# A gated recurrence and its MLP on one core: the recurrence's late chunks on 64x64 tiles only, in three steps with a VectorE copy between them, and a new order of the steps

## The chip, the cores and the metric

One NeuronCore of a Trainium2 chip runs the program. The metric is the device time of one execution in microseconds (us); before the change it is 501.38 us, the median of 3 runs (501.32 to 502.95). Engines are named TensorE (PE in the profile, its weight loads PEld), VectorE (DVE), ScalarE (ACT), GpSimd (POOL) and SyncE (SP, which issues the DMAs).

## The reference

Two stages follow each other. The first is a gated linear recurrence over 768 time steps for 4 batches of 8 heads of width 48, the second an MLP with a Mish activation over all 3072 tokens of width 384, with 2048 hidden units:

```python
# recurrence (B=4, H=8, S=768, D=48), f = sigmoid(f_logit)
for t in range(S):
    state = f[:, :, t, :, None] * state + einsum('bhd,bhe->bhde', k[:, :, t], v[:, :, t])
    y[:, :, t] = einsum('bhd,bhde->bhe', q[:, :, t], state)
x = y.transpose(0, 2, 1, 3).reshape(B * S, H * D)      # 3072 x 384
# MLP
h = x @ w_in                                            # 3072 x 2048
g = h * tanh(log1p(exp(h)))
out = g @ w_out                                         # 3072 x 384
```

## The kernel before

**The recurrence in chunks.** A chunk is 128 time steps of one batch; there are 24 (n = 0 to 23), four of which (one of each batch) make the 512 tokens of one group g of the MLP. Within a chunk the work is done in halves of 64 steps. For a chunk TensorE forms the scores of keys and queries (`score`, L525), which VectorE multiplies with a causal mask into the tiles `a` (`mask`, L532); the two states' updates from keys and values (`update`, L568), from which VectorE makes `mid` (L627) and `tmp` (L629) and GpSimd the next state (L717); and the output `y`, a sum in PSUM of what the state brings (`inter_at`, L691) and of what the masked scores bring within the chunk (`intra_at`, L699). Each of these products uses a part of TensorE's array: a row tile of 64 rows (which half of the partitions the operands lie on) and a column tile (which half of the partitions of PSUM the result goes to). Each fp32 matmul stands as two records in the trace.

**Late chunks.** From n = 9 (`MERGED`) on, that is for 15 chunks, the output of chunk n-1 and the scores and updates of chunk n are issued as one run on TensorE, in `attn2`. It is made of two steps that follow each other at once (`plan.glue(1)`): `run` issues the products `near(1 - e, e, ..., 32)` on tiles of 64 rows by 32 columns, then 16 `far` products on 64x64 tiles in turn with 16 scores; `run_on` issues the other half of `far` and scores, the updates and the products `near(e, e)`. `far` is `inter_at`, `near` is `intra_at`. `near(c, e)` works on row tile c and adds to PSUM bank `y[e]`, `far(e, ...)` works on row tile e and adds to the same bank. `y` lies in banks `at_[0]` and `at_[1]`, and so do the updates (their second halves); the scores lie in `at_[2]` (`at1`) and in `h_[lent]`, the one of the MLP's two h banks that is lent for it.

**The MLP.** For each unit u (group g, hidden block j of 128) TensorE makes h in 9 matmuls of 512 columns (`moe_in`, L261), then ScalarE, VectorE and GpSimd turn it into `gh` and `gl` (`mish`, L277 to L292; the order is exp L285, +1 L286, square L278, ln L288, exp L289, times h L290, split L292 and L282), and two units later TensorE adds 9 matmuls to the four output banks `o_` (`moe_out`, L299). The first blocks use plain fp32 (L269, L272).

**The order.** `Plan` collects all steps with an engine and a cost written by hand, packs them by a list schedule, searches for an order by repeated forward and backward packings and then by random changes of the ranks (`order`, 10 settings with 30 turns each, then `SHIFTS` = 1000 draws), and issues every engine's instructions in that order. Each engine runs its own instructions strictly in it. At the start `issue` fills TensorE's waiting time with matmuls on zeros (`idle`, L402).

Of the kernel before, what the change touches and what calls it, by code (L numbers as in the profile page):

```python
# [10 lines left out]
F32 = mybir.dt.float32  # L11
# [10 lines left out]
P = 128  # L22
# [21 lines left out]
EARLY = 24  # L44
EARLY_J = 2
WHOLE = 5
SHIFTS = 1000
MERGED = 2 * GC + 1


class Plan:
# [30 lines left out]
    def pack(self, rank, ahead, haste, back=False):  # L82
# [20 lines left out]
        forced = None  # L103
        found = dict.fromkeys(queue)
        stale = set(queue)
        transfers = shared = 0.0
        for _ in range(count):
            for e in stale:
                found[e], q, at_least = None, queue[e], free[e]
                if q:  # L110
                    at = [(max(ready[i], shared) if port[i] else ready[i], i) for i in q]
                    t0 = max(at_least, min(at)[0])
                    _, t, i = min(
                        [(rank[i] + haste * max(0.0, r - t0), max(at_least, r), i) for r, i in at if r <= t0 + ahead]
                    )
# [12 lines left out]
            end = free[e] = t + cost[i]  # L128
            if port[i]:
                shared = end  # L130
                stale.update(("dve", "pool"))
            if e == "sp" and not back:
                transfers = max(transfers, end + 650.0) + steps[i][4] / 0.27
                end = transfers - 650.0
            for a in after[i]:
                f = a if back else i
                if engine[i] == engine[a] == "pe":
                    lag = 0.0
                else:
                    lag = self.LATENCY[engine[f]]  # L140
                    if back and engine[f] == "sp":
                        lag += steps[f][4] / 0.27
                ready[a] = max(ready[a], end + lag)
                left[a] -= 1
                if not left[a]:
                    queue[engine[a]].append(a)
                    stale.add(engine[a])
        return start

    def order(self):  # L150

        count = len(self.steps)
        cost = [s[1] for s in self.steps]

        def packed(rank, *setting):
            start = self.pack(rank, *setting)
            return max(start[i] + cost[i] for i in range(count)), start

        best = None
        for setting in ((200.0, 5.0), (400.0, 10.0), (1000.0, 20.0), (200.0, 50.0), (50.0, 2.0), (0.0, 0.0), (100.0, 1.0), (100.0, 20.0), (300.0, 20.0), (600.0, 20.0)):  # L160
            rank = list(range(count))
            for _ in range(30):
                end, start = packed(rank, *setting)
                if best is None or end < best:
                    best, self.start, kept = end, start, (rank, setting)
                back = self.pack([-start[i] - cost[i] for i in range(count)], *setting, True)
                rank = [-back[i] - cost[i] for i in range(count)]
        ranks, setting = kept
        draw = random.Random(1)
        for _ in range(SHIFTS):  # L170
            spread, width = draw.choice((200, 500, 1500, 4000)), draw.choice((5e3, 2e4, 1e5, 5e5))
            left = draw.random() * best * 0.3
            rank = [r + (draw.gauss(0, spread) if left <= at < left + width else 0) for r, at in zip(ranks, self.start)]
            end, start = packed(rank, *setting)
            if end <= best:
                best, self.start, ranks = end, start, rank
        return sorted(range(count), key=lambda i: (self.start[i], i))

    def issue(self):
# [32 lines left out]
def recurrence_moe_kernel(  # L212
# [18 lines left out]
    def ctile(shape, dtype, name):  # L231
        return const.tile(shape, dtype, tag=name, name=name)
# [15 lines left out]
    ones = ctile([P, 1], F32, "ones")  # L248
    okc = ctile([P, 1], F32, "okc")
    flag = ctile([1, 1], I32, "flag")  # L250
    ends = ctile([P, NCH, NP, 1], F32, "ends")
    state = ctile([P, B, NP, 64], F32, "state")
    state0 = ctile([P, P], F32, "state0")
# [48 lines left out]
    with tc.tile_pool(name="work", bufs=1) as pool, tc.tile_pool(  # L302
# [94 lines left out]
        waits = iter([None] * 26 + [(F32R, P, GT)] * 4 + [(F32R, P, GT // 2)] * 4 + [(BF16, P, GT)] * 4 + [(F32R, 96, GT)] * 4)  # L397

        def idle():
            form = next(waits, None)  # L400
            if form is None:
                nc.tensor.matmul(zeros[:, 0:P], state0[:, 0:P], state0[:, 0:P], start=True, stop=True)  # L402
            else:
                dtype, m, n = form
                z = blank.bitcast(dtype)
                nc.tensor.matmul(zeros[0:m, 0:n], z[:, 0:m], z[:, 0:n], start=True, stop=True)


        def load_w(j):

# [92 lines left out]
        def half(e):  # L503
            return slice(64 * e, 64 * e + 64)
# [10 lines left out]
        def attn0(n, parts):  # L515
# [1 line left out]
            (_, kk_, kq, _), (_, k, q, _), _ = inputs(n)  # L517
            b, keys = taken[n]
            st = NP // parts
            sc = [quad(x) for x in (b if n < MERGED else (at1, h_[lent]))]  # L520
            if n >= MERGED:
                keys = [("at", 2), ("h", lent)]

            def score(e, c, p):
                nc.tensor.matmul(  # L525
# [31 lines left out]
        def attn2(n):  # L557
# [6 lines left out]
            keys = [("at", 0 if merged else 2), ("at", 1)]  # L564
            tmp, kt = tmp_[n % 2], ("tmp", n % 2)

            def update(p, c, e):
                nc.tensor.matmul(  # L568
                    u[c][dims(e), p].rearrange("p (r m) -> p r m", m=4)[:, :, :3],
                    kt_s[half(c), p, dims(e)], v[half(c), 2 * p + e, :, :3],  # L570
                    start=not merged, stop=True, tile_position=(64 * c, 64 * e), skip_group_check=merged,
                )

            def updates():
# [5 lines left out]
            if merged:  # L580
                attn0(n, 1)
                score, mask, reads, writes = late[n]
                old_reads, far, near, rest = outputs_of(n - 1)

                def slot(*calls):
                    for x in range(2):
                        for f, *where in calls:
                            f(*where, x)

                def scored(e, p, x):  # L590
                    score(e, x, p)

                def run():
                    for a in range(2):
                        for x in range(4):
                            for e in (1, 0):
                                near(1 - e, e, a, x, 32)

                    for p in range(NP):
                        slot((far, 0, p // 2, p % 2), (scored, 1, p))  # L600

                def run_on():
                    for p in range(NP):
                        slot((scored, 0, p), (far, 1, p // 2, p % 2))
                    updates()
                    for a in range(2):
                        slot((near, 0, 0, a), (near, 1, 1, a))

                add("pe", 890, run, ["kt", kv[0]] + reads + old_reads, [("at", 0), ("at", 1)] + writes)
                plan.glue(1)  # L610
                add("pe", 1267, run_on, ["kt", kv[0]] + reads[: 2 * NP] + old_reads, [("at", 0), ("at", 1), writes[0]])
                mask()
            elif n >= GC:
                score, mask, reads, writes = late[n]
# [16 lines left out]
                rest()  # L631

        def attn3(n):
            outputs_of(n)[3](True)

        def outputs_of(n):
            (_, _, kq, kv), (_, _, q, v), _ = inputs(n)
# [58 lines left out]
            def intra_at(c, e, a, x, m=64):  # L696
                p = 2 * a + x * m // 64
                c0 = (2 * p + e) * 64 + x * m % 64
                nc.tensor.matmul(  # L699
                    y[e][x * m : x * m + m, a, half(c)], v[half(c), c0 : c0 + m], a_[e][half(c), p, :],  # L700
                    start=(m == 32 and a == 0), stop=True, skip_group_check=True,
                )

            def rest(alone=False):
# [48 lines left out]
            return reads, inter_at, intra_at, rest  # L753


        def start(n):
# [301 lines left out]
```

## Time and profile before

| what | value |
|---|---|
| median of 3 runs | 501.38 us (501.32 to 502.95) |
| the profiled execution's own time | 501.84 us |
| its span, first to last instruction | 500.1 us |
| PE busy | 487.8 us (98%) |
| PEld busy | 390.5 us (78%) |
| ACT busy | 360.0 us (72%) |
| DVE busy | 336.5 us (67%) |
| POOL busy | 143.7 us (29%) |
| granted TensorE clock, mean | 0.996 |

The profile shows one execution. The profiled execution took 501.84 us, of which the span of its instructions is 500.1 us; what is read from rows is counted against these two. A busy time of TensorE holds the latency of its last matmul as well, because matmuls overlap: the distance from the start of one record to the start of the next is what a record costs in a stream, and the text works with these distances. In a timeline, a row with x32 is 32 records that follow each other, with the start of the first and the time to the end of the last.

### The profile page before, as it was taken

What the parts mean: (1) busy time and instruction counts of PE and PEld (TensorE: products, weight loads), DVE (VectorE), ACT (ScalarE), POOL (GpSimd) and SP (SyncE); (2) the same over time, 40 slices, a digit from 0 to 9 for tenths busy, and PEclk for the clock granted to TensorE, in tenths of its full rate; (3) what the DMA queues carried; (4) which work ended last, traced back from release to release, by engine and by line L of the source; (5) the groups of instructions that cost most, each with busy time, mean ns of one, the idle gap of its engine ahead of it and who ended that gap; (6) DMA issues with size and microseconds to landing.
All of it is one profiled execution on the core that took longest, in us unless ns stands there. A gap on an engine that the chain in (4) does not pass through costs nothing.

```text
span 500.1 us, 12645 instructions
## 1 busy us (share of the span) xinstructions
PE 487.8 (98%) x5270; PEld 390.5 (78%) x5270; DVE 336.5 (67%) x585; ACT 360.0 (72%) x662; POOL 143.7 (29%) x128
## 2 busy tenths in 40 slices
PE   8899999999999999999999999999999999999995
PEld 8775557887877888788888888888888888888883
DVE  5579999999968877786666675666664453545441
ACT  7789988999986876777857757767665565655550
POOL 1411210000023443443434324334323223332421
PEclk9999999999999999999999999999999999999998
DMA  7886655542402525122031131130230000010001
GB/s 249 245 259 220 219 200 188 179 170 78 122 0 87 199 102 183 75 93 84 4 118 65 47 124 34 53 118 8 78 108 1 0 2 33 22 43 0 1 0 69
DMA packets 17105, 48.46 MB, mean 97 GB/s; under 512 B 2000, under 2 KB 2000, under 8 KB 17040
## 3 DMA queue, kind: packets, MB, share of 16 engines
q1 hardware_dynamic: 17040, 47.59, 28.3%
q8 instruction: 42, 0.69, 0.6%
q14 instruction: 23, 0.19, 0.1%
HBM read 39.32 MB, written 6.29 MB: 91 GB/s over the span
## 4 chain that ended last, share of the span: by engine, by line
PE 84%; DMA 7%; DVE 4%; ACT 2%; issue 1%; SPq 0%; ACTq 0%; DVEq 0%
PE o L299 38%; PE h L261 37%; DMA raw<-ww 3%; DMA in<-qv 3%; PE at L699 2%; PE at L691 2%; PE at L525 1%; PE at L552 1%; PE at L568 1%; DMA spareh<-qv 1%; PE h L269 1%; DMA spareh<-lk 1%; DVE wt L422 1%; DVE wl L437 1%; ACT wt L419 1%
## 5 line engine op out<-in xcount | busy, mean ns | idle before, releaser
L261 PE MATMUL h<-xt,wh 128*128 128x512 f32 x546 | 171.6, 396 | 0.1
L282 POOL TENSOR_TENSOR gl<-ng,gh 128x512 fp32r<-128x512 f32 x74 | 101.9, 1378 | 194.2 <-ACT gh L292 170.5
L261 PEld LDWEIGHTS h<-xt,wh 128*128 128x128 f32 x546 | 101.2, 188 | 23.5 <-DVE ng L290 1.6
L290 DVE SCALAR_TENSOR_TENSOR ng<-ng,h 128x512 f32<-128x512 f32 x91 | 62.4, 687 | 72.4 <-ACT ng L289 71.5
L299 PE MATMUL o<-gh,wh 128*128 128x512 f32 x273 | 109.4, 401 | 0.4 <-issue 0.4
L261 PE MATMUL h<-xt,wl 128*128 128x512 f32 x273 | 107.4, 393 | 0.1
L299 PE MATMUL o<-gl,wh 128*128 128x512 f32 x273 | 107.3, 393 | 0.0
L299 PE MATMUL o<-gh,wl 128*128 128x512 f32 x273 | 106.5, 390 | 0.0
L288 ACT ACTIVATE ng<-ng,half 128x512 f32<-128x512 f32 (+1 forms) x98 | 69.8, 712 | 48.1 <-DVE ng L278 42.2
L285 ACT ACTIVATE ng<-h 128x512 f32<-128x512 f32 (+1 forms) x98 | 57.4, 586 | 38.0 <-PE h L261 36.6
L286 DVE TENSOR_SCALAR ng<-ng 128x512 f32<-128x512 f32 (+1 forms) x98 | 48.9, 499 | 51.3 <-ACT ng L285 50.8
L292 ACT ACTIVATE gh<-ng 128x512 fp32r<-128x512 f32 x91 | 56.6, 624 | 18.3 <-PE o L299 16.0
L289 ACT ACTIVATE ng<-ng 128x512 f32<-128x512 f32 (+1 forms) x98 | 60.6, 619 | 1.8
L345 POOL TENSOR_TENSOR in<-in,inv 128x512 f32<-128x512 f32 x20 | 24.8, 1242 | 125.7 <-ACT inv L491 119.1
L261 PEld LDWEIGHTS h<-xt,wl 128*128 128x128 f32 x273 | 51.3, 188 | 12.2 <-DVE wl L437 0.6
L299 PEld LDWEIGHTS o<-gl,wh 128*128 128x128 f32 x273 | 51.3, 188 | 11.8 <-DVE gl L281 0.2
L299 PEld LDWEIGHTS o<-gh,wl 128*128 128x128 f32 x273 | 51.3, 188 | 11.2 <-issue 0.6
L299 PEld LDWEIGHTS o<-gh,wh 128*128 128x128 f32 x273 | 51.3, 188 | 10.9 <-DVE ob L845 0.2
L278 DVE TENSOR_TENSOR ng<-ng 128x512 f32<-128x512 f32 x74 | 52.5, 709 | 2.1
L485 DVE TENSOR_TENSOR_SCAN inv<-gate,state 128x516 f32<-128x516 f32 x20 | 26.7, 1334 | 2.7 <-ACT gate L476 1.2
L742 ACT ACTIVATE xt<-at 128x256 fp32r<-128x256 f32 x40 | 13.5, 374 | 5.9 <-PE at L699 4.9
L419 ACT ACTIVATE wt<-raw 128x768 f32<-128x768 f32 x16 | 14.7, 919 | 3.6 <-DMA raw<-ww 3.6
(145 smaller groups left out, 572.0 us busy)
## 6 DMA issues: line engine op xcount, KB each, us to landing
in<-lk SPq DMA_DIRECT2D x18, 512.0 KB, 5.1
raw<-ww SPq DMA_DIRECT2D x12, 768.0 KB, 4.2
in<-qv SPq DMA_DIRECT2D x18, 512.0 KB, 3.7
out<-ob SPq DMA_DIRECT2D x18, 256.0 KB, 2.2
raw<-ww SPq DMA_DIRECT2D x8, 384.0 KB, 4.4
in<-lk SPq DMA_DIRECT2D x8, 256.0 KB, 3.8
in<-qv SPq DMA_DIRECT2D x8, 256.0 KB, 4.2
xt<-xt SPq DMA_DIRECT2D x15, 128.0 KB, 3.5
```

Of the source, the lines that this page charges most:

```text
L261: nc.tensor.matmul(h, w[:, a * P : (a + 1) * P], xt[:, x, a, cols], start=(n == 0), stop=(n == 3 * NK - 1))
L278: ("dve", T_DVE(w), 1, lambda: nc.vector.tensor_tensor(n, n, n, ALU.mult))
L282: ("pool", T_POOL(w), 1, lambda: nc.gpsimd.tensor_tensor(gl, g, gh.bitcast(F32), ALU.subtract))
L285: ("act", T_ACT(w, True), 0, lambda: nc.scalar.activation(n, h, AF.Exp)),
L286: ("dve", T_DVE(w / 2), 1, lambda: nc.vector.tensor_scalar(n, n, E_CAP, 1.0, ALU.min, ALU.add)),
L288: ("act", T_ACT(w, False, 1), 0, lambda: nc.scalar.activation(g, n, AF.Ln, bias=half1, scale=0.5)),
L289: ("act", T_ACT(w), 0, lambda: nc.scalar.activation(g, g, AF.Exp, scale=-1.0)),
L290: ("dve", T_DVE(w), 0, lambda: nc.vector.scalar_tensor_tensor(gw if whole else g, g, 1.0, h, ALU.subtract, ALU.mult)),
L292: ("act", T_ACT(w), 0, lambda: nc.scalar.activation(gh, g, AF.Copy)),
L299: nc.tensor.matmul(o, w, x, start=(first and i == 0), stop=(last and i == 2))
L345: add("pool" if on_pool else "dve", cost, lambda: eng.tensor_tensor(dst, x, y, ALU.mult), reads, writes, port=port)
L485: add("dve", 2 * T_DVE(w + st) - 70, lambda s=s, st=st: nc.vector.tensor_tensor_scan(inv1[:, s].rearrange("p a c -> p (a c)"), gate[:, s]. ...
```

## The change

The late chunks' run is cut into three steps, and all its products use 64x64 tiles. `carried` issues the 16 `far` products and the 8 `near(e, e)`. `scored` issues the 16 scores and the updates and follows `carried` at once on TensorE. `crossed` issues the 8 products `near(1 - e, e)`, now with 64 columns, and follows `scored` at once. Between `carried` and `crossed` stands a step of VectorE, `fence`: a copy of two numbers of `y[0]` on one partition into a new tile `mark`. It waits for `carried`, and `crossed` waits for it. The scores and the updates now share the banks `h_[lent]` and `at1`, so the mask and `mid` of the one bank, and the mask and `tmp` of the other, read from there. The first product to clear the banks `y` is `far` in place of `near`.

In `Plan`, a glued step now holds only its own engine. The search is another: one setting, 30 turns, then a list of draws by seeds, each followed by two turns. `idle` issues only its first form, and a memset of GpSimd for the other forms is gone. The diff, cut:

```diff
-SHIFTS = 1000
+SETTING = (400.0, 10.0)
+MOVES = (
+    300004, 300007, 300012, 300015, 300033, 300038, 300042, 300061, 300072, 300076, 300080, 300084, 300085,
...
+)
...
                 found[e], q, at_least = None, queue[e], free[e]
+                if e in held:
+                    q = [i for i in q if i == held[e]]
...
-            if forced is None:
-                t, i = min(f for f in found.values() if f)
-            else:
-                i = forced
-                t = max(free[engine[i]], ready[i])
-            forced = follower.get(i)
+            t, i = min(f for f in found.values() if f)
             e = engine[i]
+            held.pop(e, None)
+            if i in follower:
+                held[e] = follower[i]
...
+        plan = best = packed(list(range(count)))
+        for _ in range(29):
+            plan = turned(plan[2])
+            if plan[0] < best[0]:
+                best = plan
+        for seed in MOVES:
+            draw = random.Random(seed)
+            spread, width = draw.choice((200, 500, 1500, 4000, 8000)), draw.choice((5e3, 2e4, 1e5, 5e5))
+            end, ranks, start = best
+            left = draw.random() * 0.4 * end
+            plan = best = packed(
+                [r + (draw.gauss(0, spread) if left <= at < left + width else 0) for r, at in zip(ranks, start)]
+            )
+            for _ in range(2):
+                plan = turned(plan[2])
+                if plan[0] < best[0]:
+                    best = plan
...
-        blank = xt_[1][:, 0, 0]
-        nc.gpsimd.memset(blank.bitcast(F32), 0.0)
...
-            sc = [quad(x) for x in (b if n < MERGED else (at1, h_[lent]))]
+            sc = [quad(x) for x in (b if n < MERGED else (h_[lent], at1))]
...
-            u = [quad(at_[0] if merged else at1, NP * 64 * merged), quad(at_[1], NP * 64)]
+            u = [quad(h_[lent], NP * 64), quad(at1, NP * 64)] if merged else [quad(at1), quad(at_[1], NP * 64)]
...
-                def run():
-                    for a in range(2):
-                        for x in range(4):
-                            for e in (1, 0):
-                                near(1 - e, e, a, x, 32)
-                    for p in range(NP):
-                        slot((far, 0, p // 2, p % 2), (scored, 1, p))
-
-                def run_on():
-                    for p in range(NP):
-                        slot((scored, 0, p), (far, 1, p // 2, p % 2))
+                def carried():
+                    for c in range(2):
+                        for a in range(2):
+                            for x in range(2):
+                                for e in range(2):
+                                    far(e, c, a, x)
+                    for a in range(2):
+                        for x in range(2):
+                            for e in (1, 0):
+                                near(e, e, a, x)
+
+                def fence():
+                    nc.vector.tensor_copy(mark[64:65], y[0][64:65, 1, 63:65])
+
+                def scored():
+                    for p in range(NP):
+                        for e in range(2):
+                            for c in range(2):
+                                score(e, c, p)
                     updates()
-                    for a in range(2):
-                        slot((near, 0, 0, a), (near, 1, 1, a))
-
-                add("pe", 890, run, ["kt", kv[0]] + reads + old_reads, [("at", 0), ("at", 1)] + writes)
+
+                def crossed():
+                    for a in (1, 0):
+                        for x in (1, 0):
+                            for e in range(2):
+                                near(1 - e, e, a, x)
+
+                add("pe", 790, carried, ["kt", kv[0]] + reads + old_reads, mine + writes)
+                add("dve", 65, fence, mine, ["mark"])
+                plan.glue(2)
+                add("pe", 824, scored, ["kt", kv[0]] + reads, writes)
                 plan.glue(1)
-                add("pe", 1267, run_on, ["kt", kv[0]] + reads[: 2 * NP] + old_reads, [("at", 0), ("at", 1), writes[0]])
+                add("pe", 350, crossed, [kv[0]] + old_reads, mine)
                 mask()
...
-                    start=False, stop=False, skip_group_check=True,
+                    start=(a == 0 and c == 0), stop=False, skip_group_check=True,
...
-                    start=(m == 32 and a == 0), stop=True, skip_group_check=True,
+                    start=False, stop=True, skip_group_check=True,
```

## Rows read from the trace of the kernel before

**Rows 1.** The page, part 4: shares of the last chain by engine.

```profile
PE 84%; DMA 7%; DVE 4%; ACT 2%; issue 1%; SPq 0%; ACTq 0%; DVEq 0%
```

**Rows 2.** Busy by stage: stretch, length; PE, PEld, DVE, ACT, POOL (records); clock, DMA, GB/s.

```profile
0.00:20.00 20.00, 17.86 (x348) 16.00 (x348) 9.47 (x29) 15.31 (x37) 6.36 (x16) 1.00 0.74 240
20.00:40.00 20.00, 18.40 (x406) 14.71 (x388) 16.11 (x28) 15.59 (x39) 2.61 (x3) 1.00 0.76 238
40.00:80.00 40.00, 37.97 (x629) 23.42 (x628) 38.62 (x70) 37.43 (x74) 7.21 (x8) 1.00 0.67 229
80.00:450.00 370.00, 369.53 (x3717) 300.87 (x3716) 252.88 (x429) 268.23 (x477) 114.29 (x91) 1.00 0.23 78
```

**Rows 3.** Groups by line and shape, TensorE: count, busy time, mean of one.

```profile
L402 PE MATMUL o<-state 128*128 128x128 f32 x50 | 8.4, 329 | 1.1 <-DVE state L360 1.1
...
L699 PE MATMUL at<-a,in 64*32 64x64 f32 x480 | 6.8, 222 | 0.0
L699 PE MATMUL at<-a,in 64*64 64x64 f32 x240 | 6.7, 223 | 0.0
```

**Rows 4.** Timeline of TensorE over one late run: start, length, instruction, count.

```profile
249.81 0.40 PE L261 MATMUL h<-xt,wl 128*128 128x512 f32 x1
250.14 0.45 PE L699 MATMUL at<-a,in 64*32 64x64 f32 x32
250.53 0.27 PE L691 MATMUL at<-in,state 48*64 48x64 f32 x1
...
250.63 0.22 PE L691 MATMUL at<-in,state 48*64 48x64 f32 x1
...
251.51 0.54 PE L568 MATMUL at<-in,kt 64*48 64x48 f32 x32
251.87 0.43 PE L699 MATMUL at<-a,in 64*64 64x64 f32 x16
252.22 0.50 PE L299 MATMUL o<-gh,wh 128*128 128x512 f32 x1
252.56 0.40 PE L299 MATMUL o<-gh,wl 128*128 128x512 f32 x1
252.80 0.39 PE L299 MATMUL o<-gl,wh 128*128 128x512 f32 x1
```

**Rows 5.** Timeline of TensorE, the last chunk's output by itself.

```profile
407.71 0.46 PE L650 MATMUL at<-in,state 48*64 48x64 f32 x16
408.00 0.41 PE L650 MATMUL at<-in,mid 48*64 48x64 f32 x16
408.23 0.80 PE L662 MATMUL at<-a,in 64*64 64x64 f32 x48
```

**Rows 6.** Timeline: a matmul, and VectorE's copy of its one number.

```profile
477.15 0.19 PE L810 MATMUL at<-okc,ones 128*1 128x1 f32 x2
...
477.38 0.14 DVE L811 CAST flag<-at 1x1 int32<-1x1 f32 x1 [0.40 <-PE at L810]
```

**Rows 7.** Timeline: VectorE's end, and TensorE that waited for it.

```profile
69.54 0.40 DVE L743 TENSOR_TENSOR xt<-at,xt 128x256 fp32r<-128x256 f32 x1
...
70.00 0.69 PE L525 MATMUL at<-in 48*64 48x64 f32 x32 [0.45 <-DVE xt L743]
```

**Rows 8.** Timeline of VectorE in five of the late runs.

```profile
174.90 0.91 DVE L286 TENSOR_SCALAR ng<-ng 128x512 f32<-128x512 f32 x1 [1.05 <-ACT ng L285]
...
185.99 1.18 DVE L286 TENSOR_SCALAR ng<-ng 128x512 f32<-128x512 f32 x1 [0.83 <-ACT ng L285]
...
250.88 0.74 DVE L286 TENSOR_SCALAR ng<-ng 128x512 f32<-128x512 f32 x1 [1.23 <-ACT ng L285]
...
327.84 1.41 DVE L286 TENSOR_SCALAR ng<-ng 128x512 f32<-128x512 f32 x1 [1.22 <-ACT ng L285]
...
385.56 0.61 DVE L286 TENSOR_SCALAR ng<-ng 128x512 f32<-128x512 f32 x1 [0.88 <-ACT ng L285]
386.20 0.69 DVE L278 TENSOR_TENSOR ng<-ng 128x512 f32<-128x512 f32 x1
```

**Rows 9.** Timeline after one late run: VectorE's readers, TensorE's next h.

```profile
291.53 0.42 DVE L532 TENSOR_TENSOR a<-h,causal 128x256 f32<-128x256 f32 x1 [0.82 <-PE at L699]
...
292.83 0.35 DVE L627 TENSOR_TENSOR mid<-state,at 128x192 f32<-128x192 f32 x1
...
292.20 0.39 PE L261 MATMUL h<-xt,wh 128*128 128x512 f32 x1
```

More of the change, by code (lines that the diff above doesn't have):

```diff
@@ L153, in order @@
         cost = [s[1] for s in self.steps]
[L155 to L176, printed above, removed]
+        def packed(rank):
+            start = self.pack(rank, *SETTING)
+            return max(start[i] + cost[i] for i in range(count)), rank, start
@@ new lines, in turned @@
+        def turned(start):
+            back = self.pack([-start[i] - cost[i] for i in range(count)], *SETTING, True)
+            return packed([-back[i] - cost[i] for i in range(count)])
+        plan = best = packed(list(range(count)))
[15 more added lines that the diff above has]
+                    best = plan
@@ L177, in order @@
+        self.start = best[2]
         return sorted(range(count), key=lambda i: (self.start[i], i))
@@ L250, in recurrence_moe_kernel @@
     flag = ctile([1, 1], I32, "flag")
+    mark = ctile([P, 2], F32, "mark")
     ends = ctile([P, NCH, NP, 1], F32, "ends")
@@ L393, in fetch @@
                         )
-        blank = xt_[1][:, 0, 0]
-        nc.gpsimd.memset(blank.bitcast(F32), 0.0)
-        waits = iter([None] * 26 + [(F32R, P, GT)] * 4 + [(F32R, P, GT // 2)] * 4 + [(BF16, P, GT)] * 4 + [(F32R, 96, GT)] * 4)
         def idle():
[L400 to L406, printed above, removed]
+            nc.tensor.matmul(zeros[:, 0:P], state0[:, 0:P], state0[:, 0:P], start=True, stop=True)
         def load_w(j):
@@ L519, in attn0 @@
             st = NP // parts
-            sc = [quad(x) for x in (b if n < MERGED else (at1, h_[lent]))]
+            sc = [quad(x) for x in (b if n < MERGED else (h_[lent], at1))]
             if n >= MERGED:
-                keys = [("at", 2), ("h", lent)]
+                keys = [("h", lent), ("at", 2)]
             def score(e, c, p):
@@ L562, in attn2 @@
             merged = n >= MERGED
-            u = [quad(at_[0] if merged else at1, NP * 64 * merged), quad(at_[1], NP * 64)]
-            keys = [("at", 0 if merged else 2), ("at", 1)]
+            u = [quad(h_[lent], NP * 64), quad(at1, NP * 64)] if merged else [quad(at1), quad(at_[1], NP * 64)]
+            keys = [("h", lent), ("at", 2)] if merged else [("at", 2), ("at", 1)]
             tmp, kt = tmp_[n % 2], ("tmp", n % 2)
@@ L570, in update @@
                     kt_s[half(c), p, dims(e)], v[half(c), 2 * p + e, :, :3],
-                    start=not merged, stop=True, tile_position=(64 * c, 64 * e), skip_group_check=merged,
+                    start=True, stop=True, tile_position=(64 * c, 64 * e), skip_group_check=merged,
                 )
@@ L582, in attn2 @@
                 score, mask, reads, writes = late[n]
[L583 to L591, printed above, removed]
-                def run():
+                old_reads, y, far, near, rest = outputs_of(n - 1)
+                mine = [("at", 0), ("at", 1)]
@@ L633, in attn3 @@
         def attn3(n):
-            outputs_of(n)[3](True)
+            outputs_of(n)[4](True)
         def outputs_of(n):
@@ L692, in inter_at, with intra_at @@
                     y[e][half(x), a, half(c)], x_[dims(e), 2 * a + x, :], q[dims(e), 2 * a + x, half(c)],
-                    start=False, stop=False, skip_group_check=True,
+                    start=(a == 0 and c == 0), stop=False, skip_group_check=True,
                 )
-            def intra_at(c, e, a, x, m=64):
-                p = 2 * a + x * m // 64
-                c0 = (2 * p + e) * 64 + x * m % 64
+            def intra_at(c, e, a, x):
+                c0 = (4 * a + 2 * x + e) * 64
                 nc.tensor.matmul(
-                    y[e][x * m : x * m + m, a, half(c)], v[half(c), c0 : c0 + m], a_[e][half(c), p, :],
-                    start=(m == 32 and a == 0), stop=True, skip_group_check=True,
+                    y[e][half(x), a, half(c)], v[half(c), c0 : c0 + 64], a_[e][half(c), 2 * a + x, :],
+                    start=False, stop=True, skip_group_check=True,
                 )
@@ L751, in evict @@
                             131)
-            return reads, inter_at, intra_at, rest
+            return reads, y, inter_at, intra_at, rest
         def start(n):
```

2 lines of the change are left out of this document (1 added, 1 removed), and 13 rows, old and new, of the table MOVES.

## The prediction

> **What bounds the kernel now.** I read the chain that ended last first: 84% of it is TensorE's work, 7% DMA, 4% VectorE [rows 1]. Then the stages. From 80 to 450 us TensorE is busy for 369.53 of 370.00 us, VectorE for 252.88; the granted clock is full [rows 2]. So from 80 us on the kernel is one stream of TensorE, in which each 0.1 us taken out brings the end forward by 0.1 us, and each wait put in puts it back. Before 80 us it is another kernel: TensorE idles for 2.14, 1.60 and 2.03 us in the three stretches, 5.77 us in all, while VectorE is busy for 38.62 of the 40 us from 40 to 80 and ScalarE for 37.43 [rows 2]. There, only another order of steps could give anything. All 15 late runs lie in the saturated part, so a run is read record by record [rows 4].
>
> **What a late run costs, before and after.** The narrow products begin at 250.14 and the next kind begins at 250.53: 0.39 us. Their 32 records have a length of 0.45 together, of which 0.22 is the last one's latency, so the last starts at about 250.37, and TensorE then starts nothing for 0.16 us [rows 3, 4]. The first four 64x64 records take 0.10 us (250.53 to 250.63), the 15 further groups of four 0.88 us up to 251.51, which is 0.0587 us each; the updates 0.36; `near(e, e)` with its way out 0.35 (251.87 to 252.22) [rows 4]. Sum: 0.39 + 0.10 + 0.88 + 0.36 + 0.35 = 2.08 us.
>
> After, `carried` has 48 records, that is 12 groups of four: 0.10 for the first, 11 x 0.0587 = 0.65 for the rest. That its order of loops keeps four tiles going is shown by the last chunk, whose output is issued in this order: 32 records from 407.71 to 408.23, 0.52 us, which is 0.10 + 7 x 0.06, and the 64x64 `intra` products follow with no gap [rows 5]. `scored` has 8 groups for the scores, 0.47, and the updates, 0.36. `crossed` has 16 records, as many as `near(e, e)` before, which with its way out took 0.35. Sum: 0.10 + 0.65 + 0.47 + 0.36 + 0.35 = 1.93 us. What comes ahead of the run and the first wide matmul behind it (252.22 to 252.56) stay. So a run saves 0.15 us: it is the 0.16 us of changing from narrow to square tiles, while 16 narrow products and 8 square ones are worth the same time (0.23 us, against 4 groups at 0.0587). With 15 runs (480 narrow records at 32 a run [rows 3]) that is **-2.3 us**. The last four runs have half the updates, before and after, which changes nothing.
>
> The Trainium skill, "TensorEngine Tiling (Array Packing)", section "Instruction Overhead", says that each matmul has an overhead of about 60 cycles, so that few columns cost as much as 60. The narrow records here start 0.23 / 31 = 7 ns apart [rows 4], so the trace disagrees for tiles that run side by side; by the page's figure (25 ns at 2.4 GHz, an estimate) the 16 records fewer in each of 15 runs would give 6 us.
>
> **The fence.** Count from the first record of a run. `carried`'s last record starts at 0.10 + 10 x 0.0587 + 0.02 = 0.71 and ends at 0.93. VectorE began 0.04 us after a matmul's end when it waited for one number (477.34 to 477.38), and that copy took 0.14 [rows 6]; TensorE began 0.06 us after VectorE's end (69.94 to 70.00) [rows 7]. So `crossed` may begin at 0.93 + 0.04 + 0.14 + 0.06 = 1.17. `scored` keeps TensorE until 0.10 + 0.65 + 0.47 + 0.36 = 1.58. The cover is 0.41 us, and it holds as long as VectorE can begin the copy by 1.38 after the run's first record.
>
> No row shows the fence in place, so I lay it into VectorE's sequence of before. Of the 15 runs, 11 have VectorE between two instructions in time, as the one at 385.56 (L286 ends at 386.17, 1.35 after its run's first record). In four, L286 ends too late: at 175.81, 187.17, 251.62 and 329.25, which is 1.65, 2.01, 1.48 and 2.15 after their first records, late by 0.27, 0.63, 0.10 and 0.77 [rows 8]. Bounds: nothing, and 1.8 us for all four. Below nothing is excluded, since a wait only adds. The order is found anew with the fence in it, so these four places will not stay; but the long L286 will turn up somewhere, so I take one late run of the size of the two long ones, **+0.7 us**. The copies themselves are 15 x 0.14 = 2.1 us on VectorE, which has 117 us free from 80 to 450 [rows 2]; queued behind the fence there are L278 and the masks, which wait at most for `carried`'s end.
>
> **The lent bank.** The updates now lie in `h_[lent]` too, so it comes free after the mask and `mid`, not after the mask alone. In three runs the next h follows 0.7 us behind the run, as at 292.20; the mask ends at 291.95 and `mid`, put right behind it, would end at about 292.22, so TensorE would start about 0.07 late [rows 9]. In the other runs 2 us or more lie between, or the other bank is used. **+0.2 us** at most, which I take; with `mid` where it stands now (292.83) it would be 1.0 us in such a run, the upper bound.
>
> **The order, the fillers, the memset.** Only the first 80 us can gain. There are 5.77 us of idle TensorE and some of the 8.4 us of fillers, of which L402 is the only line seen [rows 2, 3]; the removed forms of `idle` never ran, so taking them out costs and gives nothing, and the memset stood on GpSimd, which has 13.6 of the first 20 us free [rows 2]. From 40 to 80 us VectorE has 1.38 us free; an order can't take more than that out of a stretch whose work is the same. It could as well lose: bounds -3 (half of the 5.77) to +2 (the idle of 40 to 80 once more). I take half of the 1.38, **-0.7 us**.
>
> **Sum.** -2.3 + 0.7 + 0.2 - 0.7 = -2.1 us. The profiled execution took 501.84 (its span of 500.1 and 1.7 around it, which stays), so 499.7; the median of before is 0.46 lower than that, so **499.3 us**.
>
> **The rivals.**
>
> *Everything is hidden and the start gains more.* No fence is late, the lent bank is free in time, and the start gives 1.4 to 3 us: 501.4 - 2.3 - 1.4 = 497.7, down to 496.1. For it: 11 of 15 places are in time already. Against: VectorE has little room in the start.
>
> *The gain is given back.* The four late places keep their size (+1.8), the lent bank costs its 0.2 and the order nothing: 501.4 - 2.3 + 2.0 = 501.1. This is also what comes out if the change of tiling isn't gone but turns up as a pause at `crossed`, which is the first product of the run to follow a wait: 0.16 in 15 runs would eat the 2.3.
>
> *Slower: the fence queues behind L278.* VectorE takes its instructions in order; before, it stood idle for 0.82 us with a mask at its head that waited for TensorE [rows 9]. The Trainium skill says the same of the queue ("TensorE: Matmul & The Clock Gate", section "Architectural detail: the array is 16x 32x32, not 1x 128x128": ScalarE and VectorE are strict first in, first out), and that speaks against a fence. If the packed order puts L278 ahead of the fence, as both stand ready when `carried` ends, VectorE is free at 386.89 in place of 386.17, 2.07 after the first record, 0.69 late [rows 8]. In all 15 runs that is 10.4 us: 501.4 - 2.3 + 10.4 = 509.5. It decides from a mean delay of 0.15 us a run; at five of the 15 runs it is 502.5.
>
> *Narrow matmuls are bound by their number.* If a narrow record cost what a square one does (14.7 ns), a run would save 0.15 + 0.23 us and the kernel 5.7 us: 495.7. The trace speaks plainly against it (7 ns). This is the page's rule of above.
>
> **How the numbers follow.** A measurement of this kernel can tell about 0.5%, 2.5 us, from no change. The forecast's own case, with the fence between 0 and 1.8 and the order within 1 us, and the lent bank's 0.2, has 0.50 and spans 497.6 to 501.4; of it 0.20 lie below 498.9. Hidden with a better start has 0.20, given back 0.18 (501.1, same), slower 0.10, bound by number 0.02. Faster by over 0.5%: 0.20 + 0.20 + 0.02 = 0.42. Slower: of the slower case all, 0.10. Same: 0.30 + 0.18 = 0.48. The range leaves out the slowest case and the lower end of the fast one: 496.8 to 502.0.
>
> **What would show it.** In the timeline of a late run: no record of 32 columns, four products side by side all through, about 1.93 us from the first record to the first wide one, and `crossed` directly behind the updates; each gap there is the fence, and VectorE's copy in the same window tells what was ahead of it. Late h records with an idle time put down to `mid` would show the lent bank. TensorE's idle time before 80 us, against 5.77, shows what the order did. I am wrong if the runs take 2.08 us or more, if the gaps at `crossed` sum to over 2 us, or if the start moves by more than 2 us.

## The result, and the profile after

The changed kernel is slower: 505.66 us (median of 5 runs, 504.69 to 507.98) against 501.76 us (5 runs, 501.32 to 502.95); the ratio is 1.0089 with a 95% interval of 1.0065 to 1.0114. Forecast were 499.3 and a range of 496.8 to 502.0. Its profiled execution took 507.98 us, with a span of 506.2; it is the longest of the five, so times are compared by medians and single stretches by rows.

The page after, part 1, and the chain by engine:

```profile
PE 494.6 (98%) x5030; PEld 392.4 (78%) x5030; DVE 333.6 (66%) x600; ACT 360.3 (71%) x662; POOL 137.8 (27%) x127
...
PE 85%; DVE 6%; ACT 4%; DMA 2%; issue 1%; SPq 0%; ACTq 0%; DVEq 0%
```

TensorE has 240 records fewer and is busy for 7 us more. First the late runs, since the forecast is about them. A run of after on TensorE (start, length, instruction, count), which answers to [rows 4]:

```profile
258.95 0.40 PE L320 MATMUL o<-gl,wh 128*128 128x512 f32 x1
259.27 0.46 PE L708 MATMUL at<-in,state 48*64 48x64 f32 x16
259.56 0.41 PE L708 MATMUL at<-in,mid 48*64 48x64 f32 x16
259.79 0.41 PE L715 MATMUL at<-a,in 64*64 64x64 f32 x16
...
260.85 0.43 PE L715 MATMUL at<-a,in 64*64 64x64 f32 x16
261.20 0.73 PE L282 MATMUL h<-xt,wh 128*128 128x512 f32 x2
```

`crossed` begins 260.85 - 259.27 = 1.58 us after the run's first record and the first wide matmul 1.93 us after it, both as worked out, to the last digit. Counted over all 15 runs, from the first record to the first wide matmul behind it, it is 31.20 us before and 28.94 after. VectorE in the same window, and all 15 fences (engine, count, shortest, median and longest in ns; what they waited for):

```profile
260.27 0.16 DVE L608 COPY mark<-at 1x2 f32<-1x2 f32 x1 [1.17 <-PE at L715]
```

```profile
L608 DVE COPY mark<-at x15: 157/157/157, 156.1 to 396.3; 1x2 f32<-1x2 f32 x15
its engine sat idle before it (us, times) until:
  PE at L715: 15.7, 13
```

The copy ends at 260.43, 0.42 us before `crossed`. In 13 of 15 runs the profile has VectorE idle ahead of it until TensorE is done, and in all 15 it starts 1.0 us after the run's first record (the run at 155.07 has it at 156.07), well before the 1.38 at which it would cost. So the runs save what was forecast, and the fence costs nothing. The loss is elsewhere. The last pieces of the chain that ended last, before (start, length, instruction, count):

```profile
479.61 2.06 PE o L299 x9
481.67 2.06 PE h L261 x9
483.73 10.32 PE o L299 x45
```

and after:

```profile
485.54 2.10 PE o L320 x9
487.64 2.10 PE h L282 x9
489.74 10.51 PE o L320 x45
```

Nine wide matmuls take 2.06 us before and 2.10 after: 0.229 and 0.233 us each. Here no recurrence is left and the order is plain, nine of a kind in turn. The difference stands already between 100 and 150 us, ahead of the late runs (0.2290 and 0.2333 on average, counted between wide matmuls that follow each other directly). Counted in the traces, the last 500 wide matmuls (first start to last start) take 118.76 us before and 120.90 after, the last 1500 take 388.04 and 392.01, though the runs among them are 31.20 - 28.94 = 2.3 us shorter. Each wide matmul became dearer. The stages of after, which answer to [rows 2]:

```profile
0.00:20.00 20.00, 18.18 (x290) 16.50 (x294) 8.64 (x27) 14.32 (x34) 4.54 (x14) 1.00 0.77 246
20.00:40.00 20.00, 17.57 (x444) 13.91 (x440) 15.35 (x28) 14.87 (x38) 4.90 (x5) 1.00 0.78 254
40.00:80.00 40.00, 38.95 (x629) 25.04 (x630) 38.24 (x70) 36.85 (x75) 7.92 (x8) 0.96 0.63 213
80.00:450.00 370.00, 369.64 (x3462) 297.10 (x3461) 250.28 (x444) 267.25 (x475) 104.90 (x89) 1.00 0.24 79
```

TensorE's idle time before 80 us is 5.30, against 5.77; but its clock is 0.96 from 40 to 80 us. From 80 to 450 it is busy as before, at the full clock. Up to the 1500th wide matmul from the end this execution has lost 2.2 us (107.84 against 105.60, counted), of which a clock of 0.96 over 40 us would be 1.6 (an estimate from that row); in the stream behind it 4.0 more are lost, net of what the runs save.

### The profile page after: what moved, and what is told of

The parts are those of the page before. It is cut to its first block, busy times and chain, and to the rows that moved or that the text cites. A ratio compares the mean times of both kernels' runs of the same rounds, so it can differ in the third digit from the quotient of the medians.

```text
span 506.2 us, 12147 instructions
## 1 busy us (share of the span) xinstructions
PE 494.6 (98%) x5030; PEld 392.4 (78%) x5030; DVE 333.6 (66%) x600; ACT 360.3 (71%) x662; POOL 137.8 (27%) x127
## 4 chain that ended last, share of the span: by engine, by line
PE 85%; DVE 6%; ACT 4%; DMA 2%; issue 1%; SPq 0%; ACTq 0%; DVEq 0%
PE h L282 37%; PE o L320 36%; PE at L708 2%; PE at L715 1%; PE at L562 1%; PE o L417 1%; PE h L535 1%; DVE wl L447 1%; DMA raw<-ww 1%; PE h L578 1%; PE h L290 1%; DVE wt L432 1%; PE at L535 1%; ACT ng L309 1%; DMA in<-qv 1%
## 5 line engine op out<-in xcount | busy, mean ns | idle before, releaser
L282 PE MATMUL h<-xt,wh 128*128 128x512 f32 x546 | 173.7, 399 | 0.3 <-DVE ng L311 0.3
L303 POOL TENSOR_TENSOR gl<-ng,gh 128x512 fp32r<-128x512 f32 x74 | 96.7, 1318 | 217.4 <-ACT gh L313 199.2
L282 PE MATMUL h<-xt,wl 128*128 128x512 f32 x273 | 108.5, 398 | 0.2 <-DVE wl L447 0.2
L307 DVE TENSOR_SCALAR ng<-ng 128x512 f32<-128x512 f32 (+1 forms) x98 | 47.0, 479 | 57.8 <-ACT ng L306 57.1
L310 ACT ACTIVATE ng<-ng 128x512 f32<-128x512 f32 (+1 forms) x98 | 60.8, 621 | 2.3
L299 DVE TENSOR_TENSOR ng<-ng 128x512 f32<-128x512 f32 x74 | 52.0, 706 | 2.1
L495 DVE TENSOR_TENSOR_SCAN inv<-gate,state 128x516 f32<-128x516 f32 x20 | 28.1, 1406 | 10.6 <-ACT gate L486 9.9
L290 PE MATMUL h<-spareh,sparel 128*128 128x256 f32 (+1 forms) x42 | 15.6, 510 | 2.4 <-DVE ob L311 2.4
```

The costliest lines, as they stand in the source:

```text
L282: nc.tensor.matmul(h, w[:, a * P : (a + 1) * P], xt[:, x, a, cols], start=(n == 0), stop=(n == 3 * NK - 1))
L299: ("dve", T_DVE(w), 1, lambda: nc.vector.tensor_tensor(n, n, n, ALU.mult))
L303: ("pool", T_POOL(w), 1, lambda: nc.gpsimd.tensor_tensor(gl, g, gh.bitcast(F32), ALU.subtract))
L307: ("dve", T_DVE(w / 2), 1, lambda: nc.vector.tensor_scalar(n, n, E_CAP, 1.0, ALU.min, ALU.add)),
L310: ("act", T_ACT(w), 0, lambda: nc.scalar.activation(g, g, AF.Exp, scale=-1.0)),
L495: add("dve", 2 * T_DVE(w + st) - 70, lambda s=s, st=st: nc.vector.tensor_tensor_scan(inv1[:, s].rearrange("p a c -> p (a c)"), gate[:, s]. ...
```

## The experiments

What the diff does to all wide matmuls is in a line that isn't quoted ahead of the prediction: `mark = ctile([P, 2], F32, "mark")`, between `flag` and `ends`. It takes 32 bytes of each partition, and all tiles behind it move. A wide matmul reads two operands from there: the weights, which a record of PEld loads, and the moving operand, which the record of PE streams past them (xt in `moe_in`, gh and gl in `moe_out`). The addresses in the two programs (bytes in a partition):

```
                 before    after
weights wh0       16512    16512     (wl0, wh1, wl1: 41088, 65664, 90240 in both)
ends             116224   116256
xt0              148928   148960     moving operand of moe_in
gh0              198080   198112     moving operand of moe_out
```

All weights lie at 128 modulo 256 (the remainder when the address is divided by 256); before, xt, gh and gl lie at 192. Their distance from the weights modulo 256 is 64 before and 96 after. In what follows "before" is the kernel before, timed beside it on the same chip, and the brackets hold the ratio to it and its 95% interval.

**1. The tile moved, each way.** The changed kernel with `mark` behind all other tiles:

```diff
-    mark = ctile([P, 2], F32, "mark")
...
         wt_ = ring("wt", 2, [P, W_TILE], I32)
+        (mark,) = ring("mark", 1, [P, 2])
```

> The changed kernel with one edit: the new tile mark is allocated behind all other tiles instead of between flag and ends, so that every other tile lies where it lay before the change. Instructions, order and sizes stay. In the trace of the changed kernel the late runs are 0.155 us shorter each, as forecast, and still the time is 4 us longer; neighbouring 512-column matmuls start 0.233 to 0.235 us apart, before 0.229, from 100 us on, also where no late run has been yet. Theory A (place): mark takes 32 bytes and moves all tiles behind it, the moving operands of the wide matmuls (xt, gh, gl) among them, from multiples of 64 bytes to odd multiples of 32; 1,600 wide matmuls x 4.5 ns are 7 us. Then the distance goes back to 0.229 and the time to about 498.5. Theory B (order): the new order lets other engines disturb TensorE more; then nothing changes: 505.7, 0.2335. Theory C (the run's new pattern slows what follows): nothing changes either.

Measured: 500.73 us, before 501.77 (ratio 0.9980, 0.9962 to 0.9998). Its chain at the end:

```profile
478.69 2.06 PE o L319 x9
480.75 2.06 PE h L281 x9
482.81 10.31 PE o L319 x45
```

And the kernel before with the tile alone:

```diff
     flag = ctile([1, 1], I32, "flag")
+    pad = ctile([P, 2], F32, "pad")
```

> The kernel before with one edit: an unused tile of 8 bytes a partition is allocated where the change allocates mark, so that the tiles behind it lie 32 bytes further. No instruction is added. Theory A (place): the distance of wide matmuls goes from 0.229 to 0.2335 and the time from 501.8 to about 509. Theories B (order) and C (the run's pattern): no change, 501.8.

Measured: 507.31 us, before 501.77 (1.0122, 1.0100 to 1.0144).

```profile
484.21 2.10 PE o L300 x9
486.31 2.10 PE h L262 x9
488.41 10.51 PE o L300 x45
```

Theory A holds both ways: without the shift the changed kernel gains 4.9 us (505.66 to 500.73), with it the kernel before loses 5.5. Orders and runs (B and C) are out as causes of the loss. The sizes are smaller than 7 us. The last 1500 wide matmuls take 5.0 us more with the pad (393.01 against 388.04, counted). Those of them that follow each other directly, some 1430, start 0.2335 us apart against 0.2292, which is 6.1 us; 1.1 us of it comes back, since TensorE waits less between the others.

**2. Which distance.** `mark` in its place, but larger; the copy still writes two numbers. First 64 bytes:

```diff
-    mark = ctile([P, 2], F32, "mark")
+    mark = ctile([P, 16], F32, "mark")
...
-                    nc.vector.tensor_copy(mark[64:65], y[0][64:65, 1, 63:65])
+                    nc.vector.tensor_copy(mark[64:65, 0:2], y[0][64:65, 1, 63:65])
```

> The changed kernel with mark in its place but 64 bytes wide, of which the copy still writes two numbers: the tiles behind it lie 64 bytes further than before the change, on multiples of 64 again. Theory A with a grain of 64 bytes: as with mark behind everything, about 498.5 and 0.229. Theory A with a grain of 128 bytes or more, or any shift being harmful: it stays near 505.7. Theories B and C: 505.7.

Measured: 505.52, before 501.77 (1.0070, 1.0048 to 1.0093), with 2.10 for nine. So a multiple of 64 isn't enough. Then weights and all else moved by 64 bytes alike, in the kernel before:

```diff
+    ctile([P, 16], F32, "pad")
     first_w = [ctile([P, HF, W_TILE], F32R, f"w{hl}0") for hl in "hl"]
```

> The kernel before with an unused 64 bytes in front of the weights: weights and moving operands lie 64 bytes further alike, so their distance stays and only their own places move. With mark 64 bytes wide the moving operands moved by 64 and the weights did not, and the time was 505.5. If the distance between weights and moving operand decides: 501.8. If the moving operand's own place modulo 128 decides: about 505.5 to 506.

Measured: 502.04, before 501.59 (1.0011, 0.9998 to 1.0025).

```profile
479.31 2.06 PE o L300 x9
481.37 2.06 PE h L262 x9
483.43 10.32 PE o L300 x45
```

The moving operands lie where they were slow with 64 bytes, and are fast, because the weights moved too: the distance counts, not the place. The same with 128 bytes ([P, 32]):

> The changed kernel with mark in its place but 128 bytes wide, of which the copy writes two numbers: everything behind it lies 128 bytes further than before the change. If the grain of the place is 128 bytes: about 500.7, as with mark behind all other tiles, and 0.229. If any shift against the place of before is harmful, or the grain is larger: about 505.5.

Measured: 505.56, before 501.59 (1.0083, 1.0066 to 1.0099). And with 512, 256, 192 and 384 bytes:

> The changed kernel with mark in its place but 512 bytes wide. So far the moving operands are slow when they lie 32, 64 or 128 bytes further from the weights than before, and fast when weights and moving operands move by 64 together. Theory D (distance): what counts is the distance from weights to moving operands modulo some period, since TensorE reads both at once. With a period of 512 bytes (a block of 128 weights): 0.229 and about 500.7. With a longer period, or if only the one distance of before is good: about 505.5.

> The same with mark 256 bytes wide. Theory D with a period of 256 bytes: 0.229, 500.7. With a period of 512: anything between 498 and 507, and with 512 it is back at 500.7.

> The same with mark 192 bytes wide: another distance. It tells whether the distance of before is a narrow good place (then about 505.5 here as with 32, 64 and 128) or the distances differ in steps (then another value between 498 and 507).

> The same with mark 384 bytes wide, as 128 bytes the other way under a period of 512. If the distance of before is a narrow good place: about 505.5. If good places lie a half period to one side: about 500.7 or better.

Measured, before 501.77 in each: 512 bytes 500.92 (0.9976, 0.9959 to 0.9992); 256 bytes 500.77 (0.9987, 0.9960 to 1.0015); 192 bytes **497.93** (0.9926, 0.9905 to 0.9946); 384 bytes 507.30 (1.0096, 1.0064 to 1.0128). The end of the chain with 256 bytes, with 384, and with 192:

```profile
481.92 10.31 PE o L320 x45
```

```profile
489.36 10.52 PE o L320 x45
```

```profile
475.84 2.04 PE o L320 x9
477.88 2.04 PE h L282 x9
479.92 10.21 PE o L320 x45
```

The period is 256 bytes, and there is a place better than that of before: 0.227 us a matmul. Between it and the place of before, with 224 bytes:

> The changed kernel with mark in its place but 224 bytes wide: a distance of 32 modulo 256, between the best place found (192 bytes, 0: 497.9) and the one of before (256 bytes, 64: 500.8). If the good places form one range: 498 to 501. If there are single good places: about 505.5.

Measured: 508.41, before 501.86 (1.0101, 1.0047 to 1.0154), 2.10 for nine. This run's start was worse as well (TensorE idle for 3.2 us at one wait in the first 45 us), so its 508.4 isn't the place alone. The good places don't form a range. All of them, by distance:

| distance modulo 256 | kernels (bytes moved) | nine wide matmuls | time |
|---|---|---|---|
| 0 | changed (192); before (192) | 2.04 | 497.9; 499.7 |
| 32 | changed (224) | 2.10 | 508.4 |
| 64 | before (0); before, all by 64; changed (0, 256, 512) | 2.06 | 501.8; 502.0; 500.7, 500.8, 500.9 |
| 96 | changed as it is (32); before (32) | 2.10 | 505.7; 507.3 |
| 128 | changed (64) | 2.10 | 505.5 |
| 192 | changed (128, 384) | 2.10 | 505.6, 507.3 |

160 and 224 were not tried.

**3. Whose place.** In the kernel before, 32 bytes between xt and ng, so that gh and gl lie at a distance of 96 and xt at 64:

```diff
         xt_ = ring("xt", 2, [P, 2, NP, GT], F32R)
+        ring("pad", 1, [P, 2])
```

> The kernel before with an unused 32 bytes between xt and ng: xt and all tiles in front of it stay, the moving operand of the second matrix product (gh, gl) and what VectorE, ScalarE and GpSimd work on (ng, ob, raw, wt) lie 32 bytes further. Theory A1 (each wide matmul is slowed by the place of its own moving operand): L261, which reads xt, stays 0.229 apart, L299, which reads gh and gl, goes to 0.2335; about 800 x 4.5 ns = 3.7 us, 505.4. Theory A2 (it is the place of the other engines' tiles, which disturb TensorE's reads): both lines go to 0.2335, 507.3. Theory A3 (it is the small tiles or the recurrence's ones in front): neither moves, 501.8.

Measured: 504.64, before 501.59 (1.0059, 1.0043 to 1.0076).

```profile
472.07 2.07 PE h L261 x9
474.14 2.10 PE o L299 x9
476.24 2.07 PE h L261 x9
486.97 10.51 PE o L299 x45
```

L299, which reads gh and gl, takes the slow 2.10, L261 with its xt at the old distance 2.07, near the old 2.06: A1 for the main part. That L261 rises by 0.01 at all has no cause shown. Then 32 bytes in front of xt and 96 behind it:

```diff
+        ring("pad", 1, [P, 2])
         xt_ = ring("xt", 2, [P, 2, NP, GT], F32R)
+        ring("fill", 1, [P, 24])
```

> The kernel before with an unused 32 bytes in front of xt and 96 behind it: only xt lies 32 bytes off, the tiles behind it are 128 further. Theory A1 (own moving operand): L261 goes to 0.2335 and L299 stays 0.229, about 505.4, if 128 bytes are a whole grain. Theory A2 (other engines' tiles): both stay, 501.8. If 128 bytes isn't a whole grain, L299 moves too.

Measured: 507.47, before 501.59 (1.0120, 1.0103 to 1.0137).

```profile
486.98 2.10 PE h L261 x9
489.08 10.51 PE o L299 x45
```

Both lines are slow, since 128 bytes isn't a whole period: xt lies at 96, gh and gl at 192. It says the same as the table.

**4. What the change is worth at one place.** The kernel before with 192 bytes (`pad` of experiment 1 as [P, 48]):

> The kernel before with an unused 192 bytes where the change allocates mark, no other edit. The changed kernel with 192 bytes there ran in 497.9, with the wide matmuls 0.2275 us apart. If the place alone makes the difference: 0.2275 here too, 1,600 x 1.6 ns = 2.6 us less than 501.8, 499.2; then the change by itself is worth 1.0 to 1.3 us at this place as at the old one. If the good place needs the new order: 501.8.

Measured: 499.73, before 501.86 (0.9952, 0.9927 to 0.9976), with 2.04 for nine. So the place by itself is worth 2.1 us, and the change at this place 499.73 - 497.93 = 1.8 us; at the old place it was 501.77 - 500.73 = 1.0 us. The 1.8 compares two chips: by the ratios to before (0.9926 and 0.9952) it is 1.3, and their intervals overlap. In the traces the last 1500 wide matmuls take 385.29 and 384.25 us here, 1.0 less with the change, and 388.04 and 386.49 at the old place, 1.5 less (counted).

**5. The order apart from the run.** The changed kernel with `mark` behind all others and the old search (10 settings, 1000 draws) in place of the new:

> The changed kernel with mark behind all other tiles and with the search of the kernel before (10 settings of 30 turns, then 1000 draws) in place of the new one; the three-step run, the fence and the rule that a glued step holds only its own engine stay. It tells what the new search is worth by itself, with the places of before. If the new order is worth nothing: the same as the kernel with mark behind all others. If the runs save 2.3 us and nothing else moves: 501.8 - 2.3 = 499.5. If theory B holds and the new order is what costs: about 499.5 here, and 505.7 with the new search and mark behind all others.

Measured: 502.43, before 501.77 (1.0021, 1.0000 to 1.0043). Its ten executions lie between 501.31 and 505.43: the three longest have a mean granted clock of 0.988, the others 0.992 to 0.997. And the reverse, the old run with the new packing and its draws:

> The kernel before with the new packing and the new search, its list of draws included; the late runs stay in two steps with the narrow tiles, there is no mark, all tiles lie as before. The step up to which TensorE's waiting time is filled is moved by two steps, to the third of the first output products. If the new order is worth 1.7 us by itself, as the difference between the two searches with the new run says (502.4 to 500.7): 500.7 + 2.3 = 503.0 here, since only the runs are missing. If the draws fit only the steps that they were found with: anything from 502 to 506, with the difference in the first 80 us.

Measured: 504.18, before 501.86 (1.0050, 1.0027 to 1.0073). What TensorE waited for longest, in the first:

```profile
PE h L269 <- DVE ob L290: 3.9, 1, 3.9
```

and in the second:

```profile
PE at L588 <- DMA in<-qv: 1.5, 1, 1.5
PE h L281 <- DVE ob L310: 1.5, 1, 1.5
```

At the old distance the four corners are: old run and old search 501.8, new run and old search 502.4, old run and new search 504.2, new run and new search 500.7. The new run gains 3.5 us under one search and under the other nothing (0.6 more, an interval that just reaches no change), while in every trace with it the 15 runs are 2.3 us shorter. The loss of the two mixed corners lies ahead of the runs: the 1500th wide matmul from the end starts at 107.96 in the first and 107.86 in the second, against 105.60 before (counted). So each search result brings its own start, and both mixed ones are over 2 us worse than that of before; neither search is better by itself. The edit of the second also moves the step up to which waits are filled, which this corner doesn't tell apart from the search.

Where this went in the kernel with `mark` behind all others can be read. Stretches around 40 us of that kernel (columns as in [rows 2]):

```profile
38.00:40.00 2.00, 0.63 (x3) 0.58 (x4) 2.00 (x4) 1.88 (x5) 0.00 (x0) 1.00 0.75 253
40.00:42.00 2.00, 2.00 (x7) 1.58 (x6) 2.00 (x6) 2.00 (x5) 0.93 (x1) 0.59 0.40 49
42.00:44.00 2.00, 2.00 (x9) 1.15 (x9) 2.00 (x5) 1.97 (x6) 0.25 (x1) 0.55 0.84 350
```

and of before:

```profile
40.00:42.00 2.00, 1.32 (x4) 0.49 (x3) 1.88 (x6) 1.91 (x7) 0.32 (x1) 1.00 0.81 262
```

TensorE waits there for 2.05 us for L310 (0.68 before), and the granted clock then falls to 0.59 and 0.55 over two stretches, which mixes the full 2.4 GHz with 1.2. Two groups of its matmuls, ahead of the wait and behind it:

```profile
33.82 1.46 PE L289 MATMUL h<-spareh,sparel 128*128 128x256 f32 x6
...
39.37 1.99 PE L289 MATMUL h<-spareh,sparel 128*128 128x256 f32 x6 [2.05 <-DVE ob L310]
```

The same six matmuls take 1.46 and 1.99 us. The clock does not fall in every execution with this wait. In that of the kernel with 256 bytes, which has the same order, it stays at 1.00 from 38 to 44 us:

```profile
39.54 1.56 PE L290 MATMUL h<-spareh,sparel 128*128 128x256 f32 x6 [2.14 <-DVE ob L311]
```

Later three of the 15 groups of transposes cost more than the usual 0.36 us from their first record to the next matmul:

```profile
282.94 0.68 DVE L868 TENSOR_SCALAR ob<-o 128x512 f32<-128x512 f32 x1
...
283.10 0.60 PE L562 MATMUL at<-ident,in 128*128 128x128 f32 x4
...
283.77 0.47 PE L319 MATMUL o<-gh,wh 128*128 128x512 f32 x1
```

```profile
302.49 0.60 PE L562 MATMUL at<-ident,in 128*128 128x128 f32 x4
302.85 0.48 PE L319 MATMUL o<-gh,wh 128*128 128x512 f32 x1
```

It is 0.67 us in the first and 0.36 in the second. The three (0.50, 0.67, 0.67) bring the 15 groups to 6.09 us, against 5.43 before: 0.7 us (counted). In the first, the weight load of the next matmul starts 0.3 us late, behind a wait for two semaphores; the one that comes last is VectorE's, whose copy out of an output bank (L868) ends at 283.62. The kernel with the old search has the same three (0.50, 0.67, 0.67), so they stand beside the new run under either search.

The last wide matmul starts at 492.72 against 493.64 before, 0.9 us earlier. With -2.3 for the runs and +0.7 for the transposes, +0.7 is left for the start and all other waits. In the two other executions with this order and distance (256 and 512 bytes) it is -0.2 and +1.1, by the same count; so a loss at the start isn't shown for this order, and a gain isn't either.

## Why the prediction was wrong, by its own steps

**The late run: right.** 2.08 to 1.93 us was worked out, and 1.93 is what the trace has. That the saving is the pause between tilings and not the number of matmuls is borne out by the same rows: 240 records fewer, and no more than 0.15 us a run. The rival that charged each narrow matmul its own time is out.

**The fence: right in mechanism, over-charged.** 0.7 us was put in, 0 came. The copy takes 0.157 us, where 0.14 was read from [rows 6]; its end was worked out as 0.93 + 0.04 + 0.14 = 1.11 after the first record, and it is 1.16. The mistake was to lay it into VectorE's old sequence [rows 8]: in the new order VectorE has ended what it did ahead of the fence in time in all 15 runs, and the long instruction L286 (L307 after) stands directly ahead of none. The slower rival, L278 (L299 after) ahead of the fence, came about in one run, and cost nothing there, since it ended 0.21 us before the copy began:

```profile
177.11 0.69 DVE L299 TENSOR_TENSOR ng<-ng 128x512 f32<-128x512 f32 x1
178.01 0.16 DVE L608 COPY mark<-at 1x2 f32<-1x2 f32 x1 [0.21 <-PE at L715]
```

**The lent bank: over-charged.** No wait of TensorE in the trace is put down to `mid` or a mask in the late runs; 0.2 was put in.

**The order: the gain did not come.** -0.7 was taken from VectorE's free 1.38 us. At equal places 0.7 us is lost in the transposes, and the start is between 0.2 better and 1.1 worse. The bounds (-3 to +2) held it. The step that failed is "Only the first 80 us can gain", read as if nothing could be lost later either; and the clock was counted as given, though an execution in which TensorE waits for 2 us in the start can pay twice, in the wait and in slower matmuls behind it (1.99 us for six, against 1.56 where the clock stayed).

**The missing term.** The decisive step is one that isn't there. The part-by-part account goes through instructions, waits, banks and the order, and takes the price of each wide matmul as fixed: "What comes ahead of the run and the first wide matmul behind it (252.22 to 252.56) stay". Each wide matmul went from 0.229 to 0.233 us. A new tile of 8 bytes was costed at nothing by not being named. It is worth +4.9 us here (505.66 against 500.73) and +5.5 on the kernel before. With it the sum closes: -2.3 (runs) + 0.7 (transposes) + 0.7 (start and other waits) + 4.9 (place) = +4.0, measured +3.9. The 0.7 of the start is what was left over in one trace, so the sum shows that nothing large is missing, and no more.

The forecast gave 0.48 to no change and 0.42 to faster; the rival on the other side had 0.10, for another reason. Without the shift the change does gain, 1.0 us where 2.1 were forecast (ratio 0.9962 to 0.9998), and 1.3 to 1.8 at the better place, which isn't clear of the noise: the runs were right in mechanism and in size, and half of what they save is lost elsewhere.

## What to carry to other kernels

A change that adds or resizes a tile moves every tile behind it, and this can cost more than the edit saves: list the addresses before and after, and give the new tile a place behind all others, or measure the placement by itself. When a stream that wasn't touched gets slower by a per cent or two all along, compare the distance of its records in a stretch where nothing else goes on, ahead of any theory on waits. And where a search orders the steps anew, measure the edit under more than one order before it is called a gain or a loss.

## What the runs showed of the hardware that was not expected

The distance in bytes between the weights and the moving operand, modulo 256, sets what a wide fp32r matmul costs in a stream: 0.227 us at 0, 0.229 at 64, 0.233 at 32, 96, 128 and 192. Moving both alike changes nothing (502.04 against 501.59, an interval that includes no change). Moving only the moving operands of one product slows mainly that product (2.10 us for nine, 2.07 in the other). TensorE loads the next weights while it streams the moving operand: over the last 400 wide matmuls before, a weight load starts 3 ns after the start of a matmul (median, counted) and takes 188 ns, and as long after the change. Two reads that meet in the memory are therefore the natural reading; but no run shows the memory itself, and why 0 and 64 are good and 32 between them is not stays open.

The best version found is the changed kernel with `mark` 192 bytes wide: 497.93 us, ratio 0.9926 (0.9905 to 0.9946) to the kernel before.
